# Any PSUM bank for any tile, omega on ScalarE's DMA queue, and a new order: one kernel of attention and two MLPs

## The chip, the core and the metric

The kernel runs on one core of a Trainium2 chip. The metric is the device time of one execution in microseconds (us); the profile is taken from one such execution, and its span runs from the first to the last instruction. TensorE is called PE here (its weight loads PEld), VectorE DVE, ScalarE ACT, GpSimd POOL, SyncE SP.

## The reference

```python
def _attn_ref(q, k, v, omega):           # 4 batches, 8 heads, 576 rows, 64 columns; omega 128 x 64
    q_s, k_s = q * D ** -0.25, k * D ** -0.25
    def phi(x):
        proj = np.einsum('bhsd,md->bhsm', x, omega)
        h = proj - np.sum(x * x, axis=-1, keepdims=True) / 2.0
        h = h - np.max(h, axis=-1, keepdims=True)
        return np.exp(h) / np.sqrt(m)
    q_p, k_p = phi(q_s), phi(k_s)
    kv, z = np.einsum('bhsm,bhsd->bhmd', k_p, v), np.sum(k_p, axis=2)
    num = np.einsum('bhsm,bhmd->bhsd', q_p, kv)
    den = np.einsum('bhsm,bhm->bhs', q_p, z)[..., None] + 1e-06
    return num / den

def _moe_ref(x, w_in, w_out):            # 2304 x 512, d_ff 2048
    h = np.maximum(x @ w_in, 0.0)
    return h * h @ w_out

def _moe2_ref(x, w_gate, w_val, w_out, rms_g):   # 2304 x 512, d_ff 1536
    xn = x / np.sqrt(np.mean(x * x, axis=-1, keepdims=True) + 1e-06) * rms_g
    g = xn @ w_gate
    return (g / (1.0 + np.exp(-g))) * (xn @ w_val) @ w_out
```

The output of the attention, its heads side by side, is the x of the first MLP, and that one's output the x of the second.

## The kernel before, in words

The program is a list of nodes. Each node is one step of one engine (`plan.add`): its engine, a function that issues its instructions, the tiles (`Buf`) that it reads and writes. `Plan.run` issues the nodes one after the other as the table `ORDER` says: each 16-bit word names a node and which of its engines does it; the word ffff is not a node but a call of `filler` (L562 to L565), two 128x256 matmuls on a tile of ones whose result nobody reads. The table `PLACES` says, for each tile that a node is the first to use, which class of slots it takes and which slot of it. Both tables were found off the chip; the costs in `plan.add` (durations, priorities) only served to find them, and are not used when the kernel is built. So what sets the order is the tables, and every engine works through its own queue strictly in the order that they give it.

PSUM has eight banks, and each bank here is one slot: three of class "t", one of class "h" and four of class "acc". A `Buf` lists the classes that it may take. The hidden products of the first MLP (`hpart`) may only take "h", which is one bank; its output sums only "acc"; the attention's tiles mostly "t", in the first batch also the others.

Batch 0 of the attention comes first and everything waits for it. It has four pairs of heads (`pair`). For each pair and each of k and q: the transposed rows come by DMA (tiles `tt`, `lt`, `tr`), PE multiplies them by the scaled omega (`features`, L661: eight matmuls with 64 rows of the array, two PSUM tiles), DVE takes row maxima out of PSUM (L668), combines them with the row norms (L615, L673), ACT takes 128-column exponentials (L680). From these PE forms k'v (L720, L723), turns q (L774), multiplies (L780, L785), DVE divides (L755, L758, L759), PE turns the result (L819, L810), and a split into a high half (ACT, L485) and a low half (DVE, L476) gives one piece of x, 128 columns of 512. Four pairs give the four pieces. Rest rows (`rest`, 64 of each batch's 576) go the same way in `rem_prep`.

The first MLP, `moe1(0)`, multiplies these four pieces (`hpart`, L895: 12 matmuls of 512 columns a unit) with units of its weight that DVE and ACT decode from 64-bit words (`decode`, L514 to L528) and split; then `ypart` (L926) adds to four output sums. The matmuls of the later batches of the attention are spread among those of the MLP. After that come a pair of batches by seven products in place of eight (L1204, L1306, L1326) and the second MLP (L1204, L1400).

omega is loaded twice, into both halves of `om2`, by SP, as all DMAs are (L470); ACT scales it into `oms` (L573), which all products of L661 need.

Matmuls come in three shapes of the array: 128 x 128 (both MLPs, the turns L774 and L819, the fill L564), 64 x 128 (L661), and 128 x 64 (L706, L720, L723, L780, L785, L810).

## Time and profile before

| | us |
|---|---|
| median of 3 runs | 945.14 |
| lowest, highest | 944.86, 945.75 |
| the profiled execution, device time | 944.95 |
| its span | 943.1 |
| PE busy | 937.4 (99%) |
| DVE busy | 726.9 (77%) |
| ACT busy | 514.8 (55%) |
| POOL busy | 119.1 (13%) |

The span is 1.8 us shorter than the device time of the same execution. PE is busy almost without a break, and the busy time counts fill as work. To see what a part of PE's queue costs one reads the distance from the start of one row to the start of the next, since the rows of matmuls overlap at their ends.

### The profile page before, as it was taken

What the parts mean: (1) busy time and instruction counts of PE and PEld (TensorE: products, weight loads), DVE (VectorE), ACT (ScalarE), POOL (GpSimd) and SP (SyncE); (2) the same over time, 40 slices, a digit from 0 to 9 for tenths busy, and PEclk for the clock granted to TensorE, in tenths of its full rate; (3) what the DMA queues carried; (4) which work ended last, traced back from release to release, by engine and by line L of the source; (5) the groups of instructions that cost most, each with busy time, mean ns of one, the idle gap of its engine ahead of it and who ended that gap; (6) DMA issues with size and microseconds to landing.
All of it is one profiled execution on the core that took longest, in us unless ns stands there. A gap on an engine that the chain in (4) does not pass through costs nothing.

```text
span 943.1 us, 16522 instructions
## 1 busy us (share of the span) xinstructions
PE 937.4 (99%) x6132; PEld 787.0 (83%) x6132; DVE 726.9 (77%) x1341; ACT 514.8 (55%) x1080; POOL 119.1 (13%) x107
## 2 busy tenths in 40 slices
PE   9999999999999999999999999999999999999998
PEld 8978878888888888888899888888888888888886
DVE  7999898867666799887878777888998637566565
ACT  5998887655676676544335657544443423333320
POOL 1313322200121001101021011000020101110020
PEclk9999999999999999999999999999999999999999
DMA  8768898898878867757898543243232323112113
GB/s 265 258 214 280 270 310 316 284 296 311 304 262 270 262 233 264 257 193 277 298 307 299 177 140 122 68 152 124 74 104 79 101 77 91 57 57 79 45 34 112
DMA packets 78385, 182.11 MB, mean 193 GB/s; under 512 B 9184, under 2 KB 13408, under 8 KB 78304
## 3 DMA queue, kind: packets, MB, share of 16 engines
q1 hardware_dynamic: 78304, 181.06, 57.8%
q8 instruction: 48, 0.79, 0.3%
q14 instruction: 33, 0.27, 0.1%
HBM read 142.49 MB, written 38.54 MB: 192 GB/s over the span
## 4 chain that ended last, share of the span: by engine, by line
PE 99%; DVE 1%; issue 0%; ACT 0%; DVEq 0%
PE acc L1204 21%; PE acc L926 12%; PE h L895 12%; PE t L1400 12%; PE t L1204 8%; PE acc L1326 5%; PE h L1204 4%; PE h L1400 4%; PE t L661 3%; PE t L1326 3%; PE h L1306 2%; PE acc L564 2%; PE t L720 2%; PE t L1306 1%; PE t L780 1%; PE t L774 1%
## 5 line engine op out<-in xcount | busy, mean ns | idle before, releaser
L1204 PE MATMUL acc<-x,wq 128*128 128x512 f32 x452 | 159.1, 390 | 0.0
L1204 PE MATMUL acc<-xa,wq 128*128 128x512 f32 x350 | 129.7, 389 | 0.0
L1222 DVE TENSOR_TENSOR cc<-acc,cc 128x512 f32<-128x512 f32 x118 | 79.4, 685 | 63.6 <-PE acc L1204 62.5
L1400 PE MATMUL t<-wq,ub 128*128 128x512 f32 x372 | 101.3, 390 | 0.0
L1204 PEld LDWEIGHTS acc<-x,wq 128*128 128x128 f32 x452 | 84.9, 188 | 17.2
L926 PE MATMUL acc<-g,wr 128*128 128x512 f32 (+1 forms) x396 | 89.2, 361 | 0.0
L1400 PEld LDWEIGHTS t<-wq,ub 128*128 128x128 f32 x372 | 69.5, 188 | 14.7 <-DVE wq L476 0.4
L485 ACT CAST wq<-wq 128x512 fp32r<-128x512 f32 x108 | 64.1, 618 | 28.0 <-DMA wq<-w2d4o 10.8
L476 DVE TENSOR_TENSOR wq<-wq 128x512 fp32r<-128x512 f32 x108 | 75.3, 709 | 4.8 <-ACT wq L485 4.6
L1204 PEld LDWEIGHTS acc<-xa,wq 128*128 128x128 f32 x350 | 65.7, 188 | 13.4
L926 PEld LDWEIGHTS acc<-g,wr 128*128 128x128 f32 x396 | 65.0, 189 | 10.5
L680 ACT ACTIVATE p<-t,sm 128x128 f32<-128x128 f32 x220 | 61.6, 398 | 19.7 <-DVE sm L673 14.5
L895 PE MATMUL h<-x,wr 128*128 128x512 f32 x264 | 69.1, 399 | 0.7 <-ACT f L910 0.7
L1408 DVE TENSOR_TENSOR oa<-t,oa 128x512 f32<-128x512 f32 x67 | 45.2, 683 | 17.4 <-PE t L1400 17.2
L895 PEld LDWEIGHTS h<-x,wr 128*128 128x128 f32 x264 | 47.9, 188 | 11.7 <-ACT f L910 1.1
L668 DVE TENSOR_REDUCE sm<-t 128x4 f32<-128x512 f32 x62 | 40.6, 684 | 20.9 <-PE t L661 20.7
L523 ACT ACTIVATE dw<-st 128x512 f32<-128x512 f32 x57 | 39.4, 696 | 15.2 <-DMA w2d4v<-dw 4.5
L528 DVE SCALAR_TENSOR_TENSOR dw<-dw,st 128x512 uint32<-128x512 uint32 x57 | 41.7, 735 | 2.8 <-ACT st L517 1.7
L1381 ACT ACTIVATE cc<-cc 128x512 f32<-128x512 f32 x36 | 22.3, 628 | 37.5 <-DVE cc L1222 37.5
L926 PE MATMUL acc<-g,wu 128*128 128x512 f32 (+1 forms) x180 | 42.6, 362 | 0.0
L910 ACT ACTIVATE f<-h 128x512 f32<-128x512 f32 (+1 forms) x48 | 25.6, 533 | 29.4 <-PE h L895 27.7
L1400 PE MATMUL t<-wq,g 128*128 128x512 f32 x126 | 41.2, 390 | 0.0
(346 smaller groups left out, 2053.6 us busy)
## 6 DMA issues: line engine op xcount, KB each, us to landing
wr<-w1d SPq DMA_DIRECT2D x70, 512.0 KB, 5.6
st<-in_w_out_dram SPq DMA_DIRECT2D x28, 512.0 KB, 4.8
w1d<-wr SPq DMA_DIRECT2D x22, 512.0 KB, 6.5
st<-in_w_in_dram SPq DMA_DIRECT2D x16, 512.0 KB, 5.4
st<-in_w_gate_dram SPq DMA_DIRECT2D x12, 512.0 KB, 4.7
st<-in_w_val_dram SPq DMA_DIRECT2D x12, 512.0 KB, 5.3
st<-y SPq DMA_DIRECT2D x18, 256.0 KB, 4.3
v<-in_v_r_dram SPq DMA_DIRECT2D x16, 260.0 KB, 4.4
```

Source lines behind the costliest of these rows:

```text
L476: return lambda: en.tensor_tensor(out=lo(), in0=src(), in1=f32(hi()), op=ALU.subtract)
L485: first = plan.add("ACT", act(n), prio, lambda: nc.scalar.copy(out=hi(), in_=src()), rd, [whi], after, pre=[blo] if blo is not bhi else [])
L528: lambda: nc.vector.scalar_tensor_tensor(out=out().bitcast(U32), in0=out().bitcast(U32), scalar=3, in1=half(st.ap, 0), op0=ALU.logical_shi ...
L668: lambda fp=fp, js=js: nc.vector.tensor_reduce(out=mx.ap[:, js], in_=fp.ap, op=ALU.max, axis=AX),
L680: nc.scalar.activation(out=pbuf.ap[:, j, :], in_=fp.ap[:, i, :], func=AF.Exp, bias=mx.ap[:, j:j + 1])
L895: nc.tensor.matmul(hb.ap[:, :n], lhsT=u.ap[:, wl, kk * P:(kk + 1) * P], rhs=xcols(j, xl, kk)(), start=(gi == 0 and ii == 0), stop=(gi == l ...
L926: nc.tensor.matmul(accs[e].ap[:, :n], lhsT=u.ap[:, w, es], rhs=x.ap[:, :n], start=(c == 0 and i == 0), stop=(c == C1 - 1 and i == 2))
L1204: nc.tensor.matmul(bank.ap[:, cols], lhsT=u.ap[:, wl, c0 + kk * P:c0 + (kk + 1) * P], rhs=x[kk][xl].ap[:, :cols.stop - cols.start], start= ...
L1222: lambda: nc.vector.tensor_tensor(out=out.ap, in0=bank.ap, in1=x.ap, op=ALU.add), [bank, x], [out])
L1326: nc.tensor.matmul(bank.ap, lhsT=us[dc].ap[:, wl, es], rhs=gs[dc, j][xl].ap, start=dc == i == 0 and (j == 1 or first), stop=dc == 1 and i ...
L1400: nc.tensor.matmul(o.ap, lhsT=x[xl].ap[:, c0:c0 + P], rhs=us[f"o{i}"].ap[:, wl, :], start=i == n == 0, stop=i == 1 and n == 2)
L1408: lambda: nc.vector.tensor_tensor(out=oa.ap, in0=o.ap, in1=oa.ap, op=ALU.add), [o, oa], [oa])
```

## The change

Four edits in the program, and new tables.

- Every `Buf` whose first class is a PSUM class may take the banks of all three classes, in that order after its own. So a hidden product of the first MLP, say, need no longer take the one bank "h".
- omega's two loads are issued by ACT (`act_queue=True`), and DVE scales omega in place of ACT.
- `eps_sb` becomes a column of a tile `small` of eight columns. A second column of it, `warm`, is written by one 128x1 exponential on ACT. It stands as the 291st of ACT's instructions.
- `FIRST` and `AHEAD` move the load priority of the first three weight units, and `dma` has another cost for small transfers. Both only served to find the tables.
- `ORDER` and `PLACES` are new throughout. The number of nodes' matmuls is the same, 5028; fill falls from 112 matmuls (56 calls) to 42 (21 calls).

```diff
+BANKS = ["t", "h", "acc"]
 ORDER = bytes.fromhex(
-    "000000150005101600170001000400070014ffffffffffffffffffffffffffffffffffffffffffffffffffffffffffff0019"
...
 PLACES = bytes.fromhex(
-    "0000408100000101024082010000020341010283010004050242068182020100030001000783400004080641020001000001"
+    "4081000000004001820101000102030283000204014081020500400102010000010001028201050600000201830300000781"
...
     def __init__(self, classes=None, view=None, ap=None):
+        if classes and classes[0] in BANKS:
+            classes = [*classes, *(c for c in BANKS if c not in classes)]
         self.classes = classes
...
+    FIRST = 3
+    AHEAD = 10.0
...
-    eps_sb = const.tile([P, 1], F32, name="eps_sb")
+    small = const.tile([P, 8], F32, name="small")
+    eps_sb, warm = small[:, :1], small[:, 1:2]
...
-    def dma(prio, outap, inap, nbytes, r=(), w=(), after=()):
+    def dma(prio, outap, inap, nbytes, r=(), w=(), after=(), act_queue=False):
+        if act_queue:
+            return plan.add("ACT", 0.6, prio, lambda: nc.scalar.dma_start(out=outap(), in_=inap()), r, w, after, tail=2.3)
         return plan.add(
-            "SP", nbytes / 311e3, prio,
+            "SP", max(0.45, nbytes / 311e3), prio,
...
-    b_om = Buf(ap=om2)
+    b_om, b_warm = Buf(ap=om2), Buf(ap=warm)
     for h in range(2):
-        dma(T0, lambda h=h: om2[h * D:(h + 1) * D, :], lambda: omega_t, 32768, w=[(b_om, h)])
+        dma(T0, lambda h=h: om2[h * D:(h + 1) * D, :], lambda: omega_t, 32768, w=[(b_om, h)], act_queue=True)
+    plan.add("ACT", 1.4, T0 + 1.0, lambda: nc.scalar.activation(out=warm, in_=f32(ones[:, :1]), func=AF.Exp), [b_late],
+             [b_warm], after=plan.nodes[-1:])
...
-    plan.add("ACT", 0.4, T0, lambda: nc.scalar.activation(out=oms, in_=om2, func=AF.Copy, scale=SCALE), [b_om], [b_oms])
+    plan.add("DVE", 0.2, T0, lambda: nc.vector.tensor_scalar(out=oms, in0=om2, scalar1=SCALE, scalar2=None, op0=ALU.mult),
+             [b_om], [b_oms])
...
-                last_split[:] = [prepare(pos, 8.08, ((w_in, w_out)[kind], c), u, lo_eng, last_split + gate)]
+                last_split[:] = [prepare(pos, 8.08 + AHEAD * (i < FIRST), ((w_in, w_out)[kind], c), u, lo_eng, last_split + gate)]
```

In the new kernel the program's lines stand 8 to 11 further down: L470 is L478 (on ACT L475), L476 is L484, L485 is L493, L564 is L572, L661 is L672, L668 is L679, L895 is L906, L926 is L937, and so on.

The new order at three places. First the very start of SP's queue, before the change (`ld` are rows for the norms, `tt`, `tr` and `lt` transposed rows for PE):

```order
L470 DMA ld_199<-in_rest_r_dram 128x512
L470 DMA om_76<-in_omega_t_dram 64x128 x2
L470 DMA tr_211<-in_rest_t_dram 128x512
L470 DMA ld_255<-in_q_r_dram 128x512
L470 DMA ld_260<-in_q_r_dram 128x512
L470 DMA tt_262<-in_q_t_dram 128x512
```

And after it, SP's queue:

```order
L478 DMA tt_199<-in_q_t_dram 128x512
L478 DMA ld_236<-in_q_r_dram 128x512
L478 DMA lt_239<-in_q_t_dram 128x512
L478 DMA tr_241<-in_rest_t_dram 128x512
L478 DMA ld_254<-in_q_r_dram 128x512
L478 DMA ld_285<-in_rest_r_dram 128x512
```

The transposed q of the first pair is now SP's first load, not its sixth, and omega's two loads are the first instructions of ACT's queue, ahead of its table load.

Second, PE's queue where the pieces of x come in; before the change (`h_993` is the first hidden product, the four x of an even number its four pieces' high halves, `wr_635` its weight):

```order
L895 MATMUL h_993<-x_817,wr_635 128x512
L895 MATMUL h_993<-x_818,wr_635 128x512
...
L564 MATMUL acc_197<-ones 128x256 x4
L819 MATMUL t_1007<-ident,xw_954 128x128 x4
...
L895 MATMUL h_993<-x_915,wr_635 128x512
L895 MATMUL h_993<-x_916,wr_635 128x512
...
L564 MATMUL acc_197<-ones 128x256 x2
L895 MATMUL h_993<-x_1008,wr_635 128x512
L895 MATMUL h_993<-x_1009,wr_635 128x512
```

And after it (x_831, x_765, x_962 and x_973 are the pieces' high halves in the order of their use, 832, 766, 963 and 974 the low ones):

```order
L906 MATMUL acc_934<-x_831,wu_676 128x512
...
L906 MATMUL acc_948<-x_831,wr_632 128x512
...
L906 MATMUL acc_934<-x_766,wu_676 128x512
...
L906 MATMUL acc_948<-x_962,wr_632 128x512
...
L906 MATMUL acc_998<-x_831,wr_884 128x512
L906 MATMUL acc_998<-x_765,wr_884 128x512
L906 MATMUL acc_998<-x_962,wr_884 128x512
L906 MATMUL acc_998<-x_973,wr_884 128x512
L906 MATMUL acc_948<-x_973,wr_632 128x512
L906 MATMUL acc_948<-x_974,wr_632 128x512
```

Three hidden products, in three banks, now take each piece as it comes; before, one did, with fill between. Ahead of the first matmul that reads the fourth piece's low half PE has 20 matmuls of hidden products, and had 10; it has 11 groups of L661's form, and had 10.

Third, PE's queue among the matmuls of the first MLP; before the change, around one group of the second batch's features:

```order
L926 MATMUL acc_1234<-g_1262,wr_1168 128x512
L926 MATMUL acc_1234<-g_1261,wr_1168 128x512
L661 MATMUL t_1406<-oms,tt_1357 128x128
L661 MATMUL t_1407<-oms,tt_1357 128x128
...
L895 MATMUL h_1374<-x_817,wr_1323 128x512
L895 MATMUL h_1374<-x_982,wr_1323 128x512
```

And after it, around another one:

```order
L906 MATMUL t_1637<-x_973,wr_1522 128x512
L791 MATMUL t_1671<-kv_84,qt_1560 64x65 x8
L796 MATMUL t_1671<-kv_84,qr_1583 64x65 x2
L791 MATMUL h_1672<-kv_84,qt_1561 64x65 x8
L672 MATMUL t_1701<-oms,lt_1549 128x128
L672 MATMUL t_1702<-oms,lt_1549 128x128
...
L937 MATMUL acc_1129<-g_1657,wu_1577 128x512
```

The group of 64 x 128 now follows one of 128 x 64 directly, so that one way out of the 512-column matmuls serves both. Counted from the fourth piece's low half to the end, the queue passes from 128 x 128 to another shape 40 times from a matmul of 512 columns before and 27 times after, and leaves a shape other than 128 x 128 50 times before and 44 times after.

## Rows read from the trace of the kernel before

**Rows 1.** The page: busy time by engine, and the chain that ended last.

```profile
PE 937.4 (99%) x6132; PEld 787.0 (83%) x6132; DVE 726.9 (77%) x1341; ACT 514.8 (55%) x1080; POOL 119.1 (13%) x107
PE 99%; DVE 1%; issue 0%; ACT 0%; DVEq 0%
```

**Rows 2.** Waits of PE: us in total, times, longest.

```profile
PE acc L564 <- DVE ones L548: 1.1, 1, 1.1
PE h L895 <- ACT f L910: 0.7, 1, 0.7
PE t L1204 <- DVE cs L1222: 0.2, 1, 0.2
```

**Rows 3.** Stretches: length, busy PE, PEld, DVE, ACT, POOL, clock, DMA share, GB/s.

```profile
20.00:40.00 20.00, 20.00 (x416) 18.28 (x412) 19.64 (x60) 19.98 (x63) 3.98 (x4) 1.00 0.79 271
40.00:60.00 20.00, 19.31 (x170) 15.59 (x167) 18.58 (x43) 18.50 (x43) 5.14 (x5) 1.00 0.64 217
60.00:100.00 40.00, 40.00 (x356) 32.62 (x354) 35.98 (x77) 35.91 (x79) 14.50 (x11) 1.00 0.83 267
```

**Rows 4.** Line L564, the fill: duration in ns, first and last start.

```profile
L564 PE MATMUL acc<-ones x112: 276/283/582, 1.1 to 48.9; 128*128 128x256 f32 x112
```

**Rows 5.** Order of time, PE: start, us, instruction.

```profile
1.05 6.15 PE L564 MATMUL acc<-ones 128*128 128x256 f32 x30 [1.05 <-DVE ones L548]
...
13.66 3.38 PE L564 MATMUL acc<-ones 128*128 128x256 f32 x26
16.97 1.16 PE L661 MATMUL acc<-oms,tt 64*128 64x128 f32 x16
18.06 1.10 PE L774 MATMUL t<-ident,p 128*128 128x128 f32 x8
...
48.98 0.86 PE L895 MATMUL h<-x,wr 128*128 128x512 f32 x3
```

**Rows 6.** Order of time, DVE, to the fourth low half (L476 at 47.79).

```profile
9.07 0.68 DVE L668 TENSOR_REDUCE sm<-acc 128x4 f32<-128x512 f32 x1
...
14.36 0.68 DVE L668 TENSOR_REDUCE sm<-t 128x4 f32<-128x512 f32 x1
14.96 0.68 DVE L668 TENSOR_REDUCE sm<-acc 128x4 f32<-128x512 f32 x1
...
19.85 0.68 DVE L615 TENSOR_REDUCE sm<-ld 128x8 f32<-128x512 f32 x1
...
47.79 0.69 DVE L476 TENSOR_TENSOR x<-t,x 128x512 fp32r<-128x512 f32 x1
48.40 0.42 DVE L525 TENSOR_SCALAR dw<-dw 128x512 f32<-128x512 f32 x1
```

**Rows 7.** Order of time, the first loads on SP and their users on ACT.

```profile
0.74 0.40 SPq L470 DMA_DIRECT2D ld<-in_rest_r_dram  x1
1.20 1.20 SPq L470 DMA_DIRECT2D om<-in_omega_t_dram  x2
...
3.63 0.63 ACT L583 ACTIVATE ld<-ld 128x512 f32<-128x512 f32 x1 [1.62 <-DMA ld<-in_rest_r_dram]
...
4.17 0.30 ACT L573 ACTIVATE oms<-om 128x128 f32<-128x128 f32 x1
```

**Rows 8.** Order of time, weight loads, among the first MLP's matmuls.

```profile
73.74 0.65 PEld L926 LDWEIGHTS acc<-g,wu 128*128 128x128 f32 x3
74.42 0.87 PEld L895 LDWEIGHTS h<-x,wr 128*128 128x128 f32 x4
75.33 0.64 PEld L926 LDWEIGHTS acc<-g,wr 128*128 128x128 f32 x3
76.32 0.97 PEld L661 LDWEIGHTS t<-oms,tt 64*128 64x128 f32 x16 [0.35 <-issue]
77.41 0.76 PEld L895 LDWEIGHTS h<-x,wr 128*128 128x128 f32 x4
```

**Rows 9.** Order of time, weight loads, single ones of L661 and the next.

```profile
19.76 0.19 PEld L661 LDWEIGHTS h<-oms,lt 64*128 64x128 f32 x1
...
19.87 0.19 PEld L661 LDWEIGHTS h<-oms,lt 64*128 64x128 f32 x1
20.18 0.31 PEld L706 LDWEIGHTS t<-ident,pr 128*64 128x64 f32 x8
```

More of the change, by code (lines that the diff above doesn't have):

```diff
@@ new lines @@
+    "001d100c001e000f0010000d0011ffffffffffffffffffffffff00311032019200120193001f00200045003700380013ffff"
+    "0048001420460047004901950072000900730076002f007700740194004a001901960030ffffffff002c002d002effff0033"
+    "0181004b004c004d00750184018200780034007d0081007900390035004301a2005d00a1004e00e60197007a0082007e0071"
+    "007b005e005a00a000360185118300ab003a008b0083007c0186005f0060006501a301af107f003b11a410a200800084005b"
+    "0088006600890085018700ac003c00a4005c00e5008c0061108a00a3003d00a5006200a61188019811990067006300cd00a7"
@@ new lines @@
+    "00860087006800af00a8003f01b001a5006400930069008d00b000ad00d9006a00b100b900a901b2009f00ae0040008e00aa"
+    "006b00e7006c00b200b301a6006d008f00ba0094006e009500b500e800b600b7009001bf003e00b401a701b300bb01c011b1"
+    "009101a801b4009200b811a900c1006f00700041004200e9010f00bc00ea01b501cb00de00bd009600c200c3015811b600eb"
+    "00ec01c101c200da009700ed019a00be009800c400ee00c500bf018a01c300c000c600ef01cc01c4009a009d019b00c8009e"
+    "01ce00cb018b018c00df01c511c601db00cc10db01b800e000dc01cd01de00cf018d018e018f119000ce01cf20d001df01dc"
@@ L218 @@
+    "0803000008090582400780438207090581010204060180414040420a00080003064301050207828203044101820340820140"
+    "80028240820005018083420a01410106074083400181838202"
 )
```

363 lines of the change are left out of this document (175 added, 188 removed).

## The prediction

> **What bounds the kernel now.** I read the busy times and the chain first: PE is busy for 937.4 us of 943.1, and 99% of the chain that ended last is PE [rows 1]. PE's own waits come to 2.0 us in three places, none after the first 55 us but one of 0.2 [rows 2]. So from there on the time is the sum of PE's queue, and an edit to any other engine is worth nothing unless it delays PE. But busy is not the same as useful: 112 of the matmuls are fill, all between 1.1 and 49 us [rows 4]. They make the start look busy. The stretches tell what bounds it: from 20 to 40 us DVE is busy for 19.64 of 20 us and ACT for 19.98, while PE fills; from 40 to 100 us both are at 90% or more beside a PE that no longer fills [rows 3]. The start is bound by DVE and ACT working through batch 0 of the attention, all the rest by PE.
>
> That gives one point to measure at: the matmul of the first MLP that reads the low half of x's fourth piece. Before, DVE ends that half as it goes on at 48.40 [rows 6], and PE, which does three matmuls on the piece from 48.98, reads it with the second at 49.2 [rows 5]. From there to the end are 943.1 - 49.2 = 893.9 us, of which 0.9 are the two waits: 893.0 of PE's queue. The new time is the new moment of that matmul, plus what then remains.
>
> **When the fourth piece is ready.** Count DVE's queue at the pace of its unbroken rows, start to start (0.60 us for a maximum over 128x512, 14.36 to 14.96 [rows 6]). Up to that half it holds 104 instructions and 38.6 us of such work; it ends at 48.4, so DVE is 9.8 us late. The lateness is made early: 5.8 us at 9.07, 8.9 at 19.85, and only 0.9 more in the 28 us after that.
>
> Why so late: the first 30 fill matmuls take 6.15 us, 0.205 each, against 0.13 for the 26 from 13.66 [rows 5]. PE starts cold, at what looks like the 1.2 GHz level though the clock column reads 1.00, and real matmuls stand behind fill that was counted at the faster pace. The first product's maximum can start only at 9.07.
>
> New order: 16 fill matmuls end at 1.05 + 16 x 0.205 = 4.35. By then the transposed q, now SP's first load, has landed: the first load was issued at 0.74 and used at 3.63 [rows 7]. omega on ACT's queue is issued beside it. Before, two issues at 1.20 fed a scaling at 4.17 [rows 7]; I take 3.6 for its landing and 0.3 for the scaling on DVE, 3.9. The first eight products take 1.09 us when warm (16.97 to 18.06 [rows 5]), so twice that cold: 6.5. DVE has done 1.8 us of work by then, so it is 4.7 us late. Three groups of products follow without fill, so the next maxima find their inputs. I followed DVE and ACT by hand from there: the first thing DVE waits for is a denominator whose k'v ACT copies behind eight exponentials, about 0.8 us, which makes 5.6. With the 0.9 that the later part added before, I take **6.5 us late**. Bounds: 4.7 (nothing more is waited for) and 9.8 (all as before).
>
> Up to the fourth low half the new DVE queue holds 106 instructions: one weight unit's decoding more, a maximum more, the scaling, fewer small copies. That is 40.5 us. So the half is ready at 40.5 + 6.5 = 47.0, and PE reads it at **47.2** (45.4 to 50.5) where it was 49.2. Fill does not stand in the way: PE's useful work up to there was 49.2 - 1.05 - 17.1 of fill (12 rows, start to start) = 31.1 us; it becomes 34.4, and fill 16 x 0.205 + 26 x 0.115 = 6.3. Together with the 1.05 at the start these make 41.7. PE will therefore wait some 5.5 us in short pieces that are not filled.
>
> **What is done by then.** With three hidden products open in three banks PE has 20 of their matmuls behind it and not 10, at 0.227 us (0.68 for three, 73.74 to 74.42 [rows 8]): 2.3 us; and one more group of features, 76.32 to 77.41 or 1.1 us with its way out [rows 8]. **3.3 us** leave the remainder. This is what any bank for any tile buys. What hides it: nothing has to, as PE had only fill there.
>
> **Changes of shape.** Three matmuls of L926 take 0.68 us when L895 follows, and 0.99 when L661's shape does (75.33 to 76.32 [rows 8]): 0.31 us for leaving the 512-column matmuls. Inside L661 pairs go by 0.11; out of it takes 0.31 (19.87 to 20.18 against 19.76 to 19.87 [rows 9]): 0.20 for the way out; I use that for 128 x 64 too. After the fourth piece the queue is PE-bound, so each counts in full. 40 - 27 = 13 x 0.31 = 4.0, and 50 - 44 = 6 x 0.20 = 1.2: **5.2 us**. Bounds: 3.5 if the ways out cost nothing and some leaving is overlapped, 6.
>
> **Edits at nothing.** The 291st instruction of ACT, a 128x1 exponential, and the wider `small` tile: ACT is at 90% there, PE does not wait for it; without that cover under 0.4 us. omega's two issues on ACT stand ahead of its table load; at 0.6 us each (1.20 for two [rows 7]) ACT is free near 3.3 and has its first square to do near 6. On SP the same 1.2 us are what brings q forward. The end of the queue keeps its form (six matmuls, an addition, a store), so the tail stays.
>
> **The sum.** Remaining: 893.0 - 3.3 - 5.2 = 884.5. Waits after the fourth piece: 0.9 as before, the same two kinds, taken as 1.0 (0 to 6). Span 47.2 + 884.5 + 1.0 = 932.7. The profiled execution's device time was 1.8 over its span and its 944.95 lies 0.2 under the median, so **934.5 us**, 1.1% less.
>
> **Rivals.**
> *The start stays as late.* If a queue of loads, or ACT, makes DVE 9.8 us late as before, PE reads the fourth piece at 50.5: 936.0 span, 937.8. For it: ACT was at 19.98 of 20 [rows 3], and the new order has more of ACT's work ahead of the piece (38.1 us by the same count, against 35.4). Against: the early lateness has a cause, fill, that is gone.
>
> *The gain is handed back in the first MLP.* From 40 to 100 us DVE and ACT are busy for some 91% [rows 3]. PE comes to this stretch 2 us sooner, holds more decoded work behind it, and saves 0.31 us at each change of shape, so it asks for weights and squares earlier. If ACT's rectifier and square of a hidden product come late each time, as the one wait of 0.7 did [rows 2], some 5 to 8 such waits give 938 to 942. Against: in the new queue DVE's count ahead of PE's falls steadily after the fourth piece.
>
> *The clock falls, and the kernel is slower.* The rows show the clock column at 1.00 throughout [rows 3], with fill in every longer gap and no unfilled wait above 1.1 us [rows 2]. The change takes away 70 of 112 fill matmuls and leaves some 5.5 us of waits in the start-up unfilled. If the granted clock goes to the 1.2 GHz level there, the 30 us of PE's work between 10 and 47 us take up to 60, of which the 5.5 us of waits cover some: up to 959. It decides from the point at which 10.6 + 5.5 = 16 us of that work run at the lower level; from there the kernel is no faster than before. Against: the waits are spread in pieces under 1 us among dense work. The Trainium skill, page "TensorE: Matmul & The Clock Gate", section "HAM oscillation — how this bites in real kernels", says that idle gaps in PE's work let the gate fall back to the lower clock and that each return is paid again. No row here shows it fall; by that rule this rival's time holds, by the rows the forecast's.
>
> *It doesn't do what it says.* If the banks are tied by their readers, so that three products cannot be open at once, the 3.3 us stay in the remainder and PE waits instead: 937.8, with the first rival's chance.
>
> **How the numbers follow.** Forecast 0.66 (931.5 to 936.5: lateness 4.7 to 8, shapes 3.5 to 6). Start as late or banks tied 0.14 (936.5 to 938.5). Handed back 0.12 (938 to 943). Clock 0.05 (947 to 959). Below 931.5, if the short waits hide better than the count allows, 0.03. The range 930 to 940 holds the first two, the last, and half of the third, some 0.85 by this count; the bounds make it no narrower. A difference of 0.2% is about what a measurement can tell from none: faster by more 0.92, within 0.02 (a clock that falls half way, or all handed back), slower 0.06.
>
> **What would show it.** Fill 42 matmuls, none after some 20 us. The first maximum near 6.5 and not 9.07. The fourth low half at 47, PE's second matmul on it at once after it. PE's waits up to then some 5 us, mostly for DVE and ACT, and about 1 us later. From that matmul to the end some 885 us, not 893. Wrong if the fourth piece comes at 50 or after (first rival), if waits of L906 or L937 for ACT add up to over 3 us (second), if the clock column shows less than 1.00 in the first 50 us (third), or if the remainder is as long as before, which would say that a change of shape costs nothing.

## The result, and the profile of the new kernel

| | before | new |
|---|---|---|
| median, us (runs) | 945.14 (5) | 936.27 (5) |
| lowest, highest | 944.85, 946.92 | 935.16, 937.38 |
| new to before, 95% interval | | 0.990 [0.9886, 0.9913] |
| the profiled execution | 944.95 | 935.47 |
| its span | 943.1 | 933.6 |
| fourth piece's low half read by PE | 49.2 | 48.6 |
| from there to the end of the span | 893.9 | 885.0 |

The forecast was 934.5, with a range of 930 to 940: the time lies in the range, 1.8 us above the forecast. The profiled execution lies 0.8 under the median, so I compare its span: 933.6 measured, 932.7 forecast.

The page of the new kernel, the busy times and the chain, to set beside [rows 1]:

```profile
PE 925.5 (99%) x6062; PEld 780.6 (84%) x6062; DVE 718.4 (77%) x1341; ACT 516.7 (55%) x1086; POOL 111.1 (12%) x102
PE 93%; ACT 4%; DVE 2%; DMA 0%; issue 0%; ACTq 0%; DVEq 0%
```

PE is as busy as it was, yet ACT now holds 4% of the chain: with less fill the chain of the start shows what the fill had hidden. PE's waits (us in total, times, longest), to set beside [rows 2]:

```profile
PE acc L572 <- DVE ones L556: 1.1, 1, 1.1
PE t L785 <- DVE sm L769: 0.8, 1, 0.8
PE acc L672 <- DVE oms L583: 0.7, 1, 0.7
PE acc L717 <- DVE xw L770: 0.4, 1, 0.4
```

These are the four longest of nine. All nine lie in the first 37 us, none behind the fourth piece; the 0.7 and the 0.2 of [rows 2] for ACT and DVE are gone. Together they are 4.2 us, 1.1 of them at the very start. The stretches of the start (length, busy PE, PEld, DVE, ACT, POOL, clock, DMA share, GB/s), to set beside [rows 3]:

```profile
0.00:10.00 10.00, 8.29 (x58) 8.00 (x60) 4.00 (x10) 2.52 (x5) 1.17 (x7) 1.00 0.75 243
10.00:20.00 10.00, 9.47 (x120) 8.49 (x120) 9.72 (x22) 10.00 (x36) 1.04 (x1) 1.00 0.94 304
20.00:30.00 10.00, 9.53 (x220) 8.46 (x218) 9.71 (x28) 10.00 (x33) 1.13 (x1) 1.00 0.73 253
30.00:40.00 10.00, 8.60 (x160) 7.30 (x158) 9.97 (x29) 9.97 (x35) 4.55 (x5) 1.00 0.71 238
40.00:50.00 10.00, 10.00 (x103) 8.52 (x102) 9.51 (x26) 10.00 (x22) 3.19 (x3) 1.00 0.91 306
```

From 10 to 50 us ACT has no free time, and DVE almost none. PE's order of time in the first 13 us, to set beside [rows 5]:

```profile
1.05 3.78 PE L572 MATMUL acc<-ones 128*128 128x256 f32 x16 [1.05 <-DVE ones L556]
5.49 0.58 PE L672 MATMUL acc<-oms,tt 64*128 64x128 f32 x1 [0.66 <-DVE oms L583]
...
10.14 0.42 PE L672 MATMUL acc<-oms,tr 64*128 64x128 f32 x1
10.35 0.38 PE L672 MATMUL t<-oms,tr 64*128 64x128 f32 x1
...
12.12 0.27 PE L672 MATMUL acc<-oms,lt 64*128 64x128 f32 x1
```

The fill's row ends at 4.83 (4.35 was forecast from a pitch of 0.205; the first start to start here is 0.38, the others are 0.214), then PE stands for 0.66 us, since omega's scaling comes at 5.21. Three groups of products then run at the slow pitch (0.21 us from pair to pair, 0.11 later), though the clock column says 1.00. The column is no evidence there: the trace's records of the granted clock begin only at 10.56 us (at 6.30 in the kernel before), which is when the pitch halves, and the column counts time without a record as full. DVE's order of time, to set beside [rows 6]:

```profile
5.21 0.23 DVE L583 TENSOR_SCALAR oms<-om 128x128 f32<-128x128 f32 x1 [4.21 <-DMA om<-in_omega_t_dram]
...
7.60 0.69 DVE L679 TENSOR_REDUCE sm<-acc 128x4 f32<-128x512 f32 x1 [0.84 <-PE t L672]
...
45.95 0.69 DVE L484 TENSOR_TENSOR x<-t,x 128x512 fp32r<-128x512 f32 x1 [0.42 <-ACT x L493]
...
47.15 0.68 DVE L484 TENSOR_TENSOR x<-h,x 128x512 fp32r<-128x512 f32 x1
```

The first maximum is at 7.60, the fourth low half done at 47.84. PE reads it as the twelfth of these thirteen matmuls, at 48.62:

```profile
46.01 3.22 PE L906 MATMUL acc<-x,wr 128*128 128x512 f32 x13
```

### The profile page after: what moved, and what is told of

Read it like the earlier page. It is cut to its first block, busy times and chain, and to the rows that moved or that the text cites. A ratio compares the mean times of both kernels' runs of the same rounds, so it can differ in the third digit from the quotient of the medians.

```text
span 933.6 us, 16368 instructions
## 1 busy us (share of the span) xinstructions
PE 925.5 (99%) x6062; PEld 780.6 (84%) x6062; DVE 718.4 (77%) x1341; ACT 516.7 (55%) x1086; POOL 111.1 (12%) x102
## 4 chain that ended last, share of the span: by engine, by line
PE 93%; ACT 4%; DVE 2%; DMA 0%; issue 0%; ACTq 0%; DVEq 0%
PE acc L1215 15%; PE t L1215 13%; PE acc L937 11%; PE t L1411 7%; PE acc L1411 6%; PE acc L1337 5%; PE h L1215 5%; PE t L906 5%; PE h L906 4%; PE t L1337 3%; PE t L672 2%; PE h L1411 2%; PE t L1317 1%; PE acc L906 1%; ACT p L691 1%; PE acc L1317 1%
## 5 line engine op out<-in xcount | busy, mean ns | idle before, releaser
L493 ACT CAST wq<-wq 128x512 fp32r<-128x512 f32 x108 | 64.2, 618 | 75.8 <-DMA wq<-w2d5o 12.8
L1215 PE MATMUL acc<-x,wq 128*128 128x512 f32 x314 | 106.0, 390 | 0.0
L484 DVE TENSOR_TENSOR wq<-wq 128x512 fp32r<-128x512 f32 x108 | 76.9, 724 | 13.9 <-ACT wq L493 13.8
L937 PE MATMUL acc<-g,wr 128*128 128x512 f32 (+1 forms) x363 | 84.6, 366 | 0.1
L1233 DVE TENSOR_TENSOR cc<-acc,cc 128x512 f32<-128x512 f32 x73 | 49.4, 686 | 37.9 <-PE acc L1215 37.5
L937 PEld LDWEIGHTS acc<-g,wr 128*128 128x128 f32 x363 | 61.5, 189 | 11.2 <-DVE g L484 0.5
L1215 PE MATMUL acc<-xa,wq 128*128 128x512 f32 x183 | 69.7, 390 | 0.0
L1215 PE MATMUL t<-x,wq 128*128 128x512 f32 x189 | 64.5, 390 | 0.0
L1411 PE MATMUL t<-wq,ub 128*128 128x512 f32 x215 | 58.9, 389 | 0.0
L691 ACT ACTIVATE p<-t,sm 128x128 f32<-128x128 f32 x180 | 52.3, 421 | 10.6 <-DVE sm L684 10.3
L484 POOL TENSOR_TENSOR g<-f,g 128x512 fp32r<-128x512 f32 (+1 forms) x25 | 29.2, 1167 | 159.6 <-DVE f L595 74.8
L1215 PE MATMUL t<-xa,wq 128*128 128x512 f32 x125 | 48.0, 389 | 0.0
L531 ACT ACTIVATE dw<-st 128x512 f32<-128x512 f32 x55 | 39.3, 716 | 15.5 <-DMA st<-in_w_val_dram 10.6
L1411 PEld LDWEIGHTS t<-wq,ub 128*128 128x128 f32 x215 | 40.2, 188 | 8.2
L1411 PE MATMUL acc<-wq,ub 128*128 128x512 f32 x162 | 45.5, 389 | 0.0
L679 DVE TENSOR_REDUCE sm<-t 128x4 f32<-128x512 f32 x52 | 34.5, 684 | 13.5 <-PE t L672 11.7
L1215 PEld LDWEIGHTS t<-x,wq 128*128 128x128 f32 x189 | 35.2, 188 | 7.2 <-DVE cc L1233 0.2
L1215 PEld LDWEIGHTS acc<-xa,wq 128*128 128x128 f32 x183 | 34.4, 188 | 6.9
L493 ACT CAST ub<-cc 128x512 fp32r<-128x512 f32 x35 | 21.5, 619 | 33.7 <-DVE cc L1395 29.4
```

The source lines that it names most:

```text
L484: return lambda: en.tensor_tensor(out=lo(), in0=src(), in1=f32(hi()), op=ALU.subtract)
L493: first = plan.add("ACT", act(n), prio, lambda: nc.scalar.copy(out=hi(), in_=src()), rd, [whi], after, pre=[blo] if blo is not bhi else [])
L531: lambda: nc.scalar.activation(out=out(), in_=hf(), func=AF.Abs, scale=65536.0), [(st, 1)], [w])
L679: lambda fp=fp, js=js: nc.vector.tensor_reduce(out=mx.ap[:, js], in_=fp.ap, op=ALU.max, axis=AX),
L691: nc.scalar.activation(out=pbuf.ap[:, j, :], in_=fp.ap[:, i, :], func=AF.Exp, bias=mx.ap[:, j:j + 1])
L937: nc.tensor.matmul(accs[e].ap[:, :n], lhsT=u.ap[:, w, es], rhs=x.ap[:, :n], start=(c == 0 and i == 0), stop=(c == C1 - 1 and i == 2))
```

## Where the 8.9 us behind the fourth piece went

I took the distances of PE's matmuls from start to start, behind the fourth low half, and split them in three: what each form needs by its own pace (0.227 us for 512 columns, 0.120 for 256, 0.109 for 128 x 128, 0.0545 for L661's form, 0.029 for 128 x 64); what is over this at a change of shape (the step across and the two behind it); and the rest, waits above all.

| | before | new | difference | forecast |
|---|---|---|---|---|
| matmuls by their own pace, us | 866.9 | 863.8 | -3.0 | -3.3 |
| changes of shape | 95 | 75 | -20 | -19 |
| what they cost, us | 19.9 | 15.7 | -4.2 | -5.2 |
| waits and the rest, us | 3.0 | 1.2 | -1.8 | +0.1 |

The three sum to 9.0; the tail behind the last matmul's start is 0.15 longer than before. A change of shape costs 0.209 us in the one trace and 0.209 in the other. That is a mean: leaving 128 x 128 costs 0.14 us for 128 x 64 and 0.20 for 64 x 128, the way back to 512-column matmuls 0.24 and 0.26, a step between the two others 0.20 to 0.23. One of the merged places, in the new kernel's weight loads (128 x 64, then 64 x 128, then 128 x 128):

```profile
55.20 0.20 PEld L821 LDWEIGHTS h<-ident,xw 128*64 128x64 f32 x4
55.47 0.97 PEld L672 LDWEIGHTS t<-oms,tt 64*128 64x128 f32 x16
56.56 0.53 PEld L937 LDWEIGHTS acc<-g,wr 128*128 128x128 f32 x3
```

## Experiments

All twelve runs in one table, with the first results of both kernels. "Fourth" is the moment at which PE reads the fourth low half, in the profiled execution; "exp" the start of ACT's first exponential. The interval is that of the ratio to the kernel before, which ran beside them. The new kernel itself ran beside the e2 runs alone, as e2_after, which is the control of the runs below; a distance of an e1 or e3 run from the new kernel is one between separate measurements, in which the kernel before had medians of 945.54 (e1), 945.45 (e2) and 945.94 (e3).

| run | median, us | ratio to before | exp | fourth | span |
|---|---|---|---|---|---|
| before | | | 10.84 | 49.2 | 943.1 |
| new | 936.27 | 0.9886 to 0.9913 | 9.39 | 48.6 | 933.6 |
| e1_fill20 | 934.69 | 0.9864 to 0.9901 | 8.83 | 48.05 | 932.9 |
| e1_omega_sp | 935.05 | 0.9866 to 0.9905 | 8.77 | 47.8 | 932.8 |
| e1_split | 935.26 | 0.9868 to 0.9903 | 8.99 | 48.1 | 934.2 |
| e1_nofill | 935.63 | 0.9871 to 0.9906 | 9.86 | 49.2 | 934.3 |
| e2_after | 936.27 | 0.9888 to 0.9914 | 9.64 | 49.7 | 934.9 |
| e2_more_changes | 943.80 | 0.9978 to 0.9996 | 8.22 | 47.4 | 940.9 |
| e2_one_open | 939.21 | 0.9917 to 0.9940 | 9.44 | 48.8 | 937.4 |
| e2_pool_squares | 939.27 | 0.9919 to 0.9943 | 9.62 | 52.5 | 937.8 |
| e3_no_squares | 936.02 | 0.9882 to 0.9909 | 9.04 | 48.9 | 934.1 |
| e3_no_sums | 935.71 | 0.9875 to 0.9905 | 10.10 | 51.5 | 936.9 |
| e3_before_fill16 | 945.46 | 0.9983 to 1.0001 | 11.33 | 48.2 | 942.7 |
| e3_start | 937.31 | 0.9894 to 0.9921 | 9.75 | 49.5 | 935.7 |

Four of these kernels have the same program and the same order up to the fourth piece: new, e2_after, e2_more_changes and e2_one_open (but for its ten moved matmuls). Their first exponential comes at 8.22 to 9.64 us and their fourth piece at 47.4 to 49.7. So from profile to profile the first exponential of one order spreads by 1.4 us and the fourth piece by 2.3, and smaller differences of "exp" or "fourth" between two runs show nothing by themselves.

### What a change of shape costs: e2_more_changes

```diff
...
+        MOVES = ((612, 288), (683, 324), ...)      # 16 pairs
+        for a, b in MOVES:                          # node a of the MLPs right behind node b
...
```

The lines left out keep each tile in the bank that the tables gave it.

> The new kernel with 16 nodes of the two MLPs' 512-column matmuls moved in the order, by about 1 us each, into places between two nodes of other shapes, all after the fourth piece: the queue's passes from one shape of the array to another go from 93 to 122 in all, the work stays the same. Theory A, a change of shape costs about 0.21 us, as the two traces' sums say (19.9 us for 95 changes before, 15.7 for 75 after): +29 x 0.21 = 6.1, total about 942. By the prediction's own prices (0.31 and 0.20 for leaving) +7.4. Rival B, changes of shape are free and the remainder shrank by waits alone: total as the control within 0.7, or a little more where a moved product is waited for.

The total is 7.5 us above the control. The remainder holds 104 changes and not 75, the 29 more that the order was given. Three of them fall together with a wait; the other 101 cost 20.9 us by the split of above, 0.207 each. These are 26 more than in the new kernel and make 5.3 us. The rest of the 8.4 us by which the remainder grew are four steps that waited, 0.5 to 0.9 us over their pace, 3.1 in all. Three of the four in the list of waits:

```profile
PE t L677 <- ACT f L926: 0.7, 1, 0.7
PE acc L796 <- ACT f L1293: 0.7, 1, 0.7
PE t L796 <- ACT kv L593: 0.6, 1, 0.6
```

Theory A holds, with 0.21 a change; the prediction's own prices were too high in sum, and the rival of free changes is out. The median is 1.8 us above theory A's 942, which the waits can account for. The waits say something more: with matmuls moved by about 1 us PE already waits for ACT in four places, so its order has little slack here.

### What the free choice of banks buys: e2_one_open

```diff
...
+        MOVES = ((440, 397), (411, 397), (410, 397))
...
```

> The new kernel with one hidden product of the first MLP open while the pieces of x come in, and not three: the second product's matmuls and the first four of the third (10 matmuls of 512 columns, 2.3 us) are moved behind the first product's last, in the order alone. Theory A, what any bank for any tile buys is work done while the pieces come: those 2.3 us move into the remainder, PE waits for the third and fourth pieces instead, fourth low half read up to 0.7 us earlier (48.0), total +1.6 to +2.3. Rival B, PE is late itself at the fourth piece, or finds other work: total within 0.7 of the control.

Total 2.9 us above the control. PE now stands where it worked before (order of time, the last column what it waited for):

```profile
47.58 0.96 PE L911 MATMUL acc<-x,wr 128*128 128x512 f32 x3 [0.21 <-DVE x L489]
48.77 0.73 PE L911 MATMUL acc<-x,wr 128*128 128x512 f32 x2 [0.23 <-DVE x L489]
```

The second row begins with the matmul on the fourth low half, at 48.77, as soon as DVE has ended it. From there to the end are 888.6 us, 3.6 more than in the new kernel: 2.3 for the ten matmuls, and one wait of 1.1 us at 94 us which the new kernel hasn't. The total is 0.6 us above theory A's range, and that wait is more than this. The piece did not come earlier, as theory A allowed, since DVE ended it when it did. So theory A holds, and the step "3.3 us done earlier" stands on two legs, this run and the -3.0 of the table.

### Omega's loads and the first fill: e1_fill20, e1_omega_sp, e1_split

```diff
# e1_fill20: two more calls of the filler in the first row of them
+        words[words.index(0xFFFF):words.index(0xFFFF)] = [0xFFFF] * 2
# e1_omega_sp: SP issues both loads of omega
-  ..., lambda: omega_t, 32768, w=[(b_om, h)], act_queue=True)
+  ..., lambda: omega_t, 32768, w=[(b_om, h)])
# e1_split: one half by SP, as its first load, the other by ACT
+  ..., lambda: omega_t, 32768, w=[(b_om, h)], act_queue=h == 1)
+        words.insert(1, words.pop(words.index(4)))
```

> The new kernel with 20 fill matmuls ahead of the first product and not 16, so that PE does not stop between the fill's end and omega's arrival (it stood for 0.66 us from 4.83 to 5.49, and its matmuls kept the slow pitch, 0.21 us a pair of 64 x 128, until 10.4; in the kernel before, whose fill did not stop, the pitch halved at 6.3). Theory A, the stop put the full pitch off: the pitch now halves at about 6.3 while the first product runs, the second and third take 1.1 us each and not 1.9 and 1.7, the fourth piece's low half is read 1 to 2 us before 48.6, total 934 to 935.5. Rival B, matmuls on 64 rows do not bring the full pitch, whatever stands before them: it still comes at about 10.4, and the total stays at 936.3 within 0.5. Rival C, DVE and ACT set the start: the pitch comes early, but the fourth piece moves by under 0.4 us.

> The new kernel with omega's two loads issued by SP again, as the second and third of its queue behind the transposed q (DVE still scales). Theory A, the loads on ACT's queue landed late (last one 5.15, with four big loads issued beside them): from SP they land near 4.2, as before where they were issued at the same 1.20; the first product starts at about 4.7 right behind the fill, the fourth piece comes about 0.8 us earlier, total about 935.5. Rival B, the edit did what it says: SP's later loads come 1.2 us later and DVE or ACT waits for the norms' rows, the first exponential later than 9.39, total 937 to 937.5.

> The new kernel with one of omega's halves as SP's first load and the other as ACT's first, so that both are issued at 0.74. Theory A: both land near 3.6, PE goes from the fill (end 4.6) into the first product without a stop, 0.85 us earlier than 5.49; the full pitch comes at about 6.3; the fourth piece 1 to 2.5 us earlier, total 934 to 935. Rival B, the transposed q, now issued 0.45 later, or the rows for the norms become what is late: first product still near 5.4, total 936.3 within 0.5. Rival C, DVE and ACT set the start: product early, fourth piece moved by under 0.4 us.

With 20 fill matmuls the full pitch is there at 6.06:

```profile
1.05 4.59 PE L573 MATMUL acc<-ones 128*128 128x256 f32 x20 [1.05 <-DVE ones L557]
5.84 0.37 PE L673 MATMUL acc<-oms,tt 64*128 64x128 f32 x1 [0.21 <-DVE oms L584]
...
6.06 0.27 PE L673 MATMUL acc<-oms,tt 64*128 64x128 f32 x1
```

From SP omega is scaled at 4.08 and not at 5.21 (order of time of DVE, and ACT's first exponential):

```profile
4.08 0.23 DVE L583 TENSOR_SCALAR oms<-om 128x128 f32<-128x128 f32 x1 [3.09 <-DMA om<-in_omega_t_dram]
8.77 1.12 ACT L691 ACTIVATE p<-acc,sm 128x128 f32<-128x128 f32 x4
```

So the edit that put omega on ACT's queue brought omega later, not earlier. From issue to landing the two loads took, in the new kernel and then in e1_omega_sp (minimum, median, maximum):

```profile
DMA to landing us min/median/max: 2.8/3.3/3.8
DMA to landing us min/median/max: 2.2/2.3/2.4
```

The spread between profiles does not explain it. In the nine profiles in which ACT issues both, they took 2.7 to 4.5 us and the second landed at 4.6 to 5.8; in the four in which SP issues both behind one big load (the kernel before, e3_before_fill16, e1_omega_sp, e3_start), 2.2 to 2.6, and it landed at 4.0 to 4.1. In e1_split omega is scaled at 3.26, and then the second transposed load is late:

```profile
PE t L673 <- DMA lt<-in_q_t_dram: 1.2, 1, 1.2
```

In all three the first exponential is 0.4 to 0.6 us ahead of the new kernel's first profile, and the fourth piece by 0.5 to 0.9 (39.2, 39.0 and 39.1 us behind it, 39.2 in the new kernel). But e2_more_changes, with the new kernel's own start, is at 8.22 and 47.4, ahead of all three. Medians fall by 1.0 to 1.6 us; the intervals still overlap with the new kernel's, so none is shown to be faster. For e1_fill20 the pitch went as theory A said and the piece only as far as the first exponential, which is nearer to rival C; omega landed later there (5.45 us) than in the new kernel's first profile (5.09), so the two fills are not compared alone. In e1_omega_sp theory A gave 0.8 us and the run 0.9. In e1_split the product came early, as theory A said, and a load late, as rival B said.

### No fill: e1_nofill

```diff
+        words = [w for w in words if w != 0xFFFF]
```

> The new kernel with all 42 fill matmuls left out (21 calls; nothing reads their result). Theory A, fill only keeps PE's pitch up and stands ahead of useful work in places: the slow pitch lasts longer, to some 12 to 15 us, the fourth piece moves by -1 to +3 us, total 935.5 to 939.5. Rival (the clock falls without fill): the slow pitch lasts through most of the first 45 us, total 945 to 959.

```profile
10.00:15.00 5.00, 2.96 (x30) 2.14 (x26) 4.86 (x12) 5.00 (x19) 0.00 (x0) 1.00 0.73 264
15.00:20.00 5.00, 3.79 (x46) 3.67 (x48) 4.35 (x10) 5.00 (x20) 1.04 (x1) 0.66 1.03 361
```

The granted clock does fall, to 0.66 from 15 to 20 us, where PE has stood for 1.5 us and stands for 1.2 more. In the rows of that stretch the pairs are 0.21 apart, the pace of the 1.2 GHz level. By the rule of the Trainium skill that the prediction cited (page "TensorE: Matmul & The Clock Gate", section "HAM oscillation — how this bites in real kernels") this was to be feared, and the trace agrees that the gate falls. But ACT is busy for 5.00 of 5 us in both rows, PE's products hide behind it, and the total is no longer than the new kernel's, and in theory A's range. So for a kernel without fill the clock rival had the mechanism right and the price wrong, by over 10 us: it counted PE's work at the slow level as if PE bounded the start.

### The new kernel again: e2_after

> The new kernel itself once more, as a control beside the others of this call and as a second profile of its start. If the stop of 0.66 us is what kept PE's pitch slow until 10.4, it shows the same again: omega lands near 5.2, slow pitch to about 10.4, fourth piece's low half read at 48.6, span 933.6. If the moment at which the full pitch comes differs from execution to execution, it comes elsewhere (between 4.6 and 9), with the first exponential near 8.8 and the fourth piece 39.3 us behind it as in the other runs of this start. Total 935 to 936.5.

Slow pitch to 10.6 again, and a fourth piece 1.1 us later than in the first profile, while the part behind it is the same (880.8 us from the fourth low half to the last matmul's start, 880.7 there). Of the 1.1, 0.25 are the first exponential. The rest is one row of DVE. First the new kernel's first profile, POOL's and DVE's rows in the order of time:

```profile
31.34 2.31 POOL L593 TENSOR_TENSOR ld<-ld 128x512 f32<-128x512 f32 x2
32.33 0.41 DVE L522 TENSOR_SCALAR st<-st 128x512 uint32<-128x512 uint32 x1
```

and the same two in e2_after, then PE's longest wait there (0.8 in the first profile):

```profile
31.62 2.05 POOL L593 TENSOR_TENSOR ld<-ld 128x512 f32<-128x512 f32 x2
32.62 1.34 DVE L522 TENSOR_SCALAR st<-st 128x512 uint32<-128x512 uint32 x1
```

```profile
PE t L785 <- DVE sm L769: 1.7, 1, 1.7
```

A shift by 0.41 us takes 1.34 beside POOL's second square, and everything behind it on DVE is late by 0.9. It has 1.34 in e2_one_open and e3_no_sums as well, 0.41 in the first profile. So a good part of the 2 us between this kernel's lowest and highest run can come from whether DVE or POOL gets there first.

The expectations give the fourth piece 39.3 us behind the first exponential; here it is 40.1.

The same happens to small operations of DVE, in both kernels. First the kernel before (POOL, DVE), then the new one's first profile (DVE, beside POOL's first square of above):

```profile
13.18 1.04 POOL L582 TENSOR_TENSOR ld<-ld 128x512 f32<-128x512 f32 x1 [11.40 <-DVE sm L668]
13.20 1.24 DVE L673 SCALAR_TENSOR_TENSOR sm<-sm,sm 128x8 f32<-128x8 f32 x2
31.44 0.96 DVE L684 SCALAR_TENSOR_TENSOR sm<-sm,sm 128x8 f32<-128x8 f32 x1
```

Each trace has 72 of these 128x8 operations, with a median of 0.17 us. Those above 0.5 us, five before and two after, all begin beside a POOL instruction and end within 0.03 us of its end. Before, two of them (1.04 us at 13.20, 0.82 at 16.27) lie in the stretch from 9.07 to 19.85 in which DVE became 3.1 us later; they make 1.5 of it. The prediction put the early lateness down to fill.

### Which engine sets the start: e2_pool_squares, e3_no_squares, e3_no_sums

```diff
# e2_pool_squares: four squares from ACT to POOL
+        for a in (23, 12, 127, 162):
+            i = words.index(0x1000 | a)
+            words[i] = a
# e3_no_squares: the same four left out
+            if n.idx in (23, 12, 127, 162):
+                n.fn = lambda: None
# e3_no_sums: DVE's sums of these four replaced
+            if plan.nodes[-1].idx in (24, 13, 128, 163):
+                plan.nodes[-1].alts = [("DVE", 0.1, lambda: nc.vector.memset(ss.ap[:, :8], 0.0))]
```

> The new kernel with four squares of rows for the norms (128x512, about 0.5 us each start to start, at 10.41, 13.93 and two at 26.30) done by POOL in place of ACT, in the same order. Theory A, ACT sets the start: it works without a gap from the first exponential (9.33) on, and the fourth piece's low half is read 39.3 us behind that in five profiles; with 2.0 us less on ACT it is read 1 to 2 us earlier than in the control, total -1 to -2. Rival B, DVE's queue sets it, as the prediction counted: DVE is as busy as ACT (9.97 of 10 us from 30 to 40), the piece moves by under 0.3 us. Rival C, POOL is late with its 1.1 us squares and holds DVE's sums up: piece later, total +0.5 to +1.

> The new kernel with four of ACT's squares of rows for the norms left out (the four that stood at 10.41, 13.93 and two at 26.30, 0.5 us each start to start), so that these norms are sums of plain values and the attention's output is another one. ACT has 2.0 us less to do ahead of the fourth piece, and nothing is added to another engine. Theory A, ACT sets the start from the first exponential on: the fourth piece's low half is read 37.3 to 38.3 us behind the first exponential and not 39.3, total -1 to -2 against the control (936.3). Rival B, DVE's queue sets it: 39.0 to 39.4 us, total within 0.4.

> The new kernel with the four DVE sums of these same squares (128x512 to 128x8, 0.60 us each start to start) replaced by settings to zero of 128x8, which leaves these norms out of the attention. DVE has about 2.1 us less ahead of the fourth piece, ACT the same as before. Theory A, ACT sets the start: fourth piece 39.0 to 39.4 us behind the first exponential, total within 0.4 of the control. Rival B, DVE sets it: 37.2 to 38.3 us, total -1 to -2. If this and the run without the squares both gain 0.5 to 1.5, the two engines hand the wait to and fro and neither sets it alone.

On POOL the squares cost 3.0 us instead of saving 1 to 2. POOL's two squares, and DVE's shift and merge beside them:

```profile
25.04 2.49 POOL L596 TENSOR_TENSOR ld<-ld 128x512 f32<-128x512 f32 x2 [6.26 <-DMA ld<-in_q_r_dram]
26.55 1.26 DVE L525 TENSOR_SCALAR st<-st 128x512 uint32<-128x512 uint32 x1
27.84 1.64 DVE L530 SCALAR_TENSOR_TENSOR st<-st 128x512 uint32<-128x512 uint32 x1
```

In the new kernel the same two forms take 0.42 and 0.69. ACT then stands idle for want of DVE, and PE waits 2.5 us in one place and 1.4 in another. That is rival C in its direction, at more than its price, and by way of DVE's own instructions. It is not all of the cost: behind these waits the granted clock fell, to half from 37.1 to 40.5 us (e2_pool_squares, then e3_no_sums, where PE had waited 1.7 us and the clock was at half from 36.3 to 39.7):

```profile
30.00:40.00 10.00, 6.91 (x108) 5.88 (x110) 9.35 (x28) 7.93 (x29) 2.65 (x3) 0.85 0.64 212
30.00:40.00 10.00, 7.92 (x135) 6.78 (x132) 9.25 (x24) 9.23 (x33) 4.07 (x4) 0.83 0.57 187
```

From the end of the last long wait to the fourth piece PE took 1.4 and 1.3 us longer there than in the new kernel. A fall at this place costs time, since PE comes to the fourth piece out of its own queue; the one in e1_nofill, at 15.7 to 19.1 us, left the fourth piece 39.3 us behind the first exponential, as without it.

With the four squares left out, and nothing put on POOL, the total stays within 0.3 us of the control; the fourth piece is 39.8 us behind the first exponential, later than either theory says. ACT gains its 2 us and waits for DVE instead (the longest wait of ACT between 10 and 50 us in e3_no_squares, and two stretches):

```profile
ACT p L693 <- DVE sm L686: 2.3, 2, 1.8
```

```profile
20.00:30.00 10.00, 8.20 (x181) 7.37 (x182) 9.93 (x25) 8.23 (x30) 2.49 (x2) 1.00 0.76 268
30.00:40.00 10.00, 8.70 (x169) 7.41 (x165) 9.97 (x29) 9.50 (x33) 2.71 (x3) 1.00 0.61 192
```

With DVE's four sums out the total stays within 0.6 us as well; its profiled execution is the slowest of its four, with the 1.34 us row, a late omega and the fall of the clock, so I read its total and not its fourth piece. Against the kernel before beside them, the two runs are 0.7 and 1.05 us better than the control was, but their intervals overlap with its interval. By the first count both gain too little for the engine that they relieve to set the start; the second is what the expectation of e3_no_sums names for two engines that hand the wait to and fro. So neither engine is shown to set the start alone: in the new kernel ACT is full from 10 to 50 us and DVE within 5% of it, and of 2 us taken from ACT most are waited for at DVE. My statement in the expectations that the fourth piece follows the first exponential by 39.3 us holds only while nothing is moved between the two.

### The first fill of the kernel before: e3_before_fill16

```diff
+        del words[words.index(0xFFFF):words.index(0xFFFF) + 7]
```

> The kernel before with 16 fill matmuls ahead of the first product and not 30; all else as it was. Theory A, the prediction's: fill ahead of the first product made the start late. The first product starts near 4.7 and not at 7.1, the first exponential near 8.5 and not at 10.78, the fourth piece's low half is read 1.5 to 2.3 us before 49.2, total 943 to 943.8. Rival B: ACT stood idle for 0.9, 1.0 and 0.7 us at 9.95, 13.53 and 16.71 in the kernel before, so other things were late too; the gain is lost in these waits, and the piece moves by under 0.6 us, total 944.6 to 945.5.

Total 0.5 us less, with an interval that includes no change. The fill ends at 4.84, and then PE waits for the loads; ACT's square of k's rows comes no earlier than before (9.32), and the first exponential not either (10.84):

```profile
5.67 0.34 PE L662 MATMUL acc<-oms,tr 64*128 64x128 f32 x1 [0.83 <-DMA tr<-in_rest_t_dram]
9.63 0.63 ACT L584 ACTIVATE ld<-ld 128x512 f32<-128x512 f32 x1 [5.19 <-DMA ld<-in_k_r_dram]
11.33 1.14 ACT L681 ACTIVATE pr<-acc,sm 128x128 f32<-128x128 f32 x4 [1.07 <-DVE sm L674]
```

The fourth piece's low half is read at 48.2, 1.0 us earlier, and half of that is lost behind it, in a wait of 0.7 us at 520 us. So the first fill was a part of the lateness at most, and not by way of the first product's maximum, as I had it: the first exponential waited for rows that SP loads late (the chain ACT's square, DVE's sum, exponential). The piece moved by half of what theory A says, the total as rival B says.

### An attempt at a better start: e3_start

```diff
# omega by SP, as in e1_omega_sp, and:
+        words.remove(0x1023)
+        words.insert(words.index(0x58) + 1, 0x1023)
```

> The new kernel with omega's loads on SP behind the transposed q, as in the run before that did so, and besides ACT's first square (it waited for its rows until 8.23 there and stood ahead of the first exponential, 8.77 start) moved behind the first four exponentials. Theory A, the time is the first exponential plus 39.3 us plus the remainder: first exponential near 8.45, fourth piece's low half at 47.5, total 934.5 to 935. Rival B, DVE then waits for that square's sum and hands the wait on to the next exponentials: no gain over the run with omega on SP (935.05).

Slower than e1_omega_sp by 2.3 us. DVE, the next in its queue, needs the square's sum, and its wait comes back to ACT and PE:

```profile
DVE sm L628 <- ACT ld L596: 1.9, 1, 1.9
```

Rival B, and more than it said. Of all the versions e1_fill20 has the lowest median, 934.69; it beats the kernel before clearly, the new one not beyond the intervals.

## Why the prediction held, step by step

- **The bound.** PE bounds all behind the fourth piece, DVE and ACT what is ahead: held. From the fourth low half to the last matmul's start are 880.5 to 881.0 us in eight of the ten profiles with the new order behind the piece, whatever the start; the other two (e1_split and e3_start) have about 1 us more of waits there.
- **When the fourth piece is read: 47.2 forecast, 48.6 measured.** This step failed in size, and in its reason. "I take 3.6 for its landing" was wrong by 1.5 us: omega landed at 5.09 and was scaled at 5.21, so the first maximum was at 7.60 and not 6.5. "The early lateness has a cause, fill, that is gone" was half of it at most: e3_before_fill16 shows loads behind it, and 1.5 us of it were two small operations of DVE beside POOL's squares. The 0.8 us that I counted for a denominator came to 0.2; another such operation beside POOL (31.44) took 0.96 and not 0.17 in its place. And the count followed DVE's queue alone. DVE ended the half at 47.84, 7.3 us late by that count where 6.5 was forecast, but PE was no longer waiting there: it came to that matmul 0.8 later, out of its own queue. PE's waits up to there, 3.0 us behind the first 1.05, were shorter than the 5.5 forecast; its work took longer, with three groups of products at the slow pitch where one was counted. The half of the first rival that said "ACT" was the better half: ACT is never free from 10 us on, and with DVE it sets the pace. The 1.4 us of this miss are less than the start's own spread (47.4 to 49.7 in the four profiles of this start), so a single profile could have met the forecast by luck.
- **What is done by then: 3.3 forecast, 3.0 measured.** Held.
- **Changes of shape: 5.2 forecast, 4.2 measured.** The count was right (19 forecast, 20 found), the price too high in sum. I added 0.31 for the step out of a 512-column matmul and 0.20 for the step back, read from weight loads; by the matmuls' own starts the step out costs 0.14 or 0.20 and the step back to 512 columns 0.24 or 0.26, in the mean 0.21 a change and 0.42 both ways. So the step out was priced too high and the step back too low. The Trainium skill, page "TensorEngine Tiling (Array Packing)", section "Key Properties", says that a change of tiling mode drains TensorE; the trace agrees in that each change costs time, 0.21 us in the mean.
- **Waits behind the piece: 1.0 forecast, 0 listed.** With the short ones they fell by 1.8 us, and no run tells why the short ones did. So the remainder came out at 885.0 where 885.5 was forecast: the changes brought 1.0 us less than forecast and the matmuls' own pace 0.3 less, the waits 1.9 more. That these nearly cancel is luck.
- **Edits at nothing.** Of the two small ones this held: the 128x1 exponential runs at 238.0 us, where no wait of PE is listed. The move of omega's loads was not at nothing, as said above.
- **The rivals.** The start did stay nearly as late (48.6 lies between the forecast's 47.2 and the rival's 50.5), for another reason than the loads or ACT alone. Nothing was handed back in the first MLP. The clock was slow for longer than I had counted, to 10.56 where I had allowed one product, without the column showing it; e1_fill20, with the full pitch from its first product, had its piece 0.6 us earlier, which is within the spread of the start. The banks are free: the new kernel has three products open in three of them, and e2_one_open shows what that is worth.
- **Median and profile.** Of the 1.8 us by which the median missed, 0.9 are the span and the rest lies between the profiled execution and the median: 0.8 measured, where the forecast named 0.2 and left it out of its sum. The new kernel's two profiles differ by 1.1 us ahead of the fourth piece and by 0.1 behind it, so the start can make as much.

Open is why the full pitch comes when it does. The trace's records of the granted clock begin with it. In four profiles PE stood for 0.66 to 1.4 us ahead of the first product before any record (new, e2_after, e2_one_open, e3_no_sums), and the records begin at 10.3 to 12.4 us. In the nine others with fill they begin at 4.4 to 7.3; PE had stood for 0.5 us or less, or, in e3_before_fill16, for 0.83 us during which the record began, at 5.30. So a longer stop and a late full pitch go together, but no run changes the stop alone.

## What to carry to other kernels

Count the lateness of a start-up on every engine that is full there, not on the one that delivers last: where two are full, what one gains the other can take back. Take several profiles of a start-up before you read a difference of 1 us from it: this one spread by 2.3. In a PE-bound part, count the changes of the array's shape and the matmuls that can be done earlier; both could be priced from the trace of before, the first to a quarter. A price is best taken from all places at once (the sum over 95 changes, kind by kind), not from one row.

## What the runs showed of the hardware

- A change between 128 x 128, 64 x 128 and 128 x 64 costs 0.21 us in the mean: 0.209 in the kernels with 95 and 75 of them, 0.207 for 101 in e2_more_changes. By kind it is 0.14 (128 x 128 to 128 x 64) to 0.26 (64 x 128 to 512 columns of 128 x 128).
- Some DVE instructions from SBUF to SBUF slow down beside POOL: a shift of 128x512 took 1.26 and 1.34 us and not 0.41, a merge 1.64 and not 0.69, while POOL squared, and a 128x8 operation 0.96 and 1.04 and not 0.17, ending as the square ended. A sum of 128x512 out of SBUF, at 29.18 in the new kernel beside POOL's work, kept its 0.68. The Trainium skill, page "SBUF — State Buffer", section "SBUF: two separate sides", says that DVE, in some modes and with two SBUF inputs, and GpSimd lock each other out for whole instructions; these rows agree, and the price is a stall of up to a POOL square's length (1.04 us alone).
- Two small loads (32 KB) landed in 2.2 to 2.6 us on SP's queue behind one big load (four profiles), and in 2.7 to 4.5 on ACT's queue, issued beside big ones (nine profiles). A queue of its own did not make them earlier.
- The clock column can read 1.00 while the pairs of matmuls go by at half pace (1 to 10 us of the new kernel). The trace holds no record of the granted clock there, and only the distance of the rows shows the pace.
- Ahead of the end of PE's work the granted clock fell to half in three profiles, behind waits of PE: of 1.5 and, as it fell, 1.2 us in e1_nofill, of 2.5 and 1.4 in e2_pool_squares, of 1.7 in e3_no_sums. In e2_after and e2_one_open it stayed at 1.00 behind a wait of 1.7.
